# Moving the local branch of an E-Branchformer layer from a phase of its own into the attention loop

## The chip, the cores and the metric

The kernel runs on one core of one Trainium2 chip. The metric is device time in microseconds of one execution. TensorE's clock is not constant: the records show it either granted in full (1.0) or at half (0.5).

## The reference, cut to what matters

The reference is one E-Branchformer layer, forward and all gradients, for 2 batches of 4000 tokens of width 144 in bf16.

```python
xa = _layernorm(x)
q, k, v = split(xa @ w_qkv)
glob = softmax(q @ k.T * D**-0.5) @ v @ w_att_out        # attention branch, 4000 x 4000 scores
h = _gelu(xa @ w_mlp_in)                                 # local branch
u, g = h[..., :D], h[..., D:]
g = _layernorm(g)
gc = sum(pad(g)[:, i:i+T] * dw_csgu[i] for i in range(5)) # depthwise convolution over tokens
loc = (u * gc) @ w_mlp_out
# ... the branches are merged, a second depthwise convolution, a residual;
# jax.vjp of all this, with grad_out, gives the gradients of x and of seven weights
```

## The kernel before

The two batches run one after the other, each in four phases: `phase_in` (norm of x, transposes, Q, B, which carries the gradient into the scores, and the whole local branch, forward and backward), `phase_attn` (scores, exp, and everything that needs the 4000 x 4000 matrices), `phase_merge_out` and `phase_dx`. `finish_weights` closes the kernel. Tokens are in 32 row blocks of 128.

In `phase_in` the local branch runs in groups of four row blocks, pipelined over groups:

```python
def norm4(dst, src, rs, tag):
    ... bn_stats, bn_aggr (VectorE); rs = pow(var + eps, -0.5) (POOL); nm = -mean * rs (VectorE)
    for j in range(4):
        nc.scalar.activation(dst[:, j, :], src[:, j, :], ACT.Identity, bias=nm[:, j:j + 1], scale=rs[:, j:j + 1])
def stB(g):
    ... # products for hs, sq = hs**2; Q; B; dug
    nc.gpsimd.tensor_scalar(a_[:], sq[:], K0 * K1, K0, op0=ALU.mult, op1=ALU.add)
    nc.vector.tensor_tensor(a_[:], a_[:], hs[:], op=ALU.mult)
    nc.scalar.activation(a_[:], a_[:], ACT.Tanh)
    ... # h, norm4(gn_t), and the gelu gradient gp_t on VectorE and POOL
def stC(g): ...  # forward convolution pc (TensorE), gc, dgc, ug; tap gradients into their own PSUM bank dW
def stD(g): ...  # backward convolution, norm gradient, dh
for s in range(NGR + 5):
    stA(s); stB(s - 1); stC(s - 3); stD(s - 5)      # bounds checks cut
```

In `phase_attn` a *unit* is a row block's quarter: 1000 keys. TensorE runs in program order; the other engines' orders are chosen by a scheduler.

```python
NP, NT = 4, 2                                        # P and Sm kept for four rows; transposes PT, ST for two
ps_s: 1 x [128, 2, 512]; ps_d: 3 banks; ps_x: 2; ps_y: 1      # all eight PSUM banks
def unit(i, c2):
    pS, pD = ...                                      # eight products of 500 columns
    nc.scalar.activation(pd, pS[:, :, 0:SC], ACT.Exp, accum_out=...)          # one exp of 1000 columns
    for h in range(2):
        nc.vector.scalar_tensor_tensor(Sm[...], pD[h][:, 0:SC], 1.0, P[...], op0=ALU.mult, op1=ALU.mult, accum_out=...)
# between units, on TensorE: y and z of row i-2 (from PT, ST) and the column sums X of a finished pair of rows
```

Of the kernel before, what the change touches and what calls it, by code (L numbers as in the profile page):

```python
# [14 lines left out]
D = 144  # L15
DR = 16
# [1104 lines left out]
def weights(k):  # L1121
# [7 lines left out]
    with tc.tile_pool(name="w_tmp", bufs=1) as tp_, tc.tile_pool(name="w_ps", bufs=2, space=PSUM) as ps:  # L1129
# [9 lines left out]
        W.Wqkv = load_k(k.w_qkv, D, 3 * D, "w_qkv_s", nc.sync)  # L1139
        W.Wo = load_k(k.w_att_out, D, D, "w_o_s", nc.scalar)  # L1140
# [3 lines left out]
        Wmh = wp.tile([128, 2, 2, D], BF, name="w_mh")  # L1144
# [4 lines left out]
        W.Wmh = Wmh  # L1149
# [40 lines left out]
        W.WoT = transpose_k(W.Wo, D, 0, D, "w_oT")  # L1190
        WlT = transpose_k(Wl, D, 0, D, "w_lT")
        WiT = transpose_k(Wi, D, 0, 2 * D, "w_iT", tp_)
        W.WmT = wp.tile([128, 2, 2, D], BF, name="w_mT")
        nc.vector.memset(W.WmT[:, :, 1, :], 0.0)
        for h in range(2):
            for cc in range(2):
                w = 128 if cc == 0 else DR
                for kt in range(2):
                    rk = 128 if kt == 0 else DR
                    pt = ps.tile([128, 128], BF, tag="tp")  # L1200
                    nc.tensor.transpose(pt[0:w, 0:rk], Wmh[0:rk, h, kt, cc * 128:cc * 128 + w], ident[0:rk, 0:rk])
                    nc.vector.tensor_copy(W.WmT[0:w, h, cc, kt * 128:kt * 128 + rk], pt[0:w, 0:rk])
# [64 lines left out]
        W.WvoT = wp.tile([128, 2, D], BF, name="w_voT")  # L1267
        W.Wvo = wp.tile([128, 2, D], BF, name="w_vo")
        for t, l, r in ((W.WvoT, W.Wo, WvT), (W.Wvo, WvT, W.Wo)):
            nc.vector.memset(t[:, 1, :], 0.0)  # L1270
            for mt in range(2):
                mw = 128 if mt == 0 else DR
                fused(lambda kt: l[:, kt, :], two(r), 1.0, mt * 128, mw, t[0:mw, mt, :])
        W.Wl = wp.tile([128, 2, D], BF, name="w_l")
        nc.vector.tensor_copy(W.Wl[:], Wl[:])

        W.UT = [W.WvoT, WlT]
        W.U = [W.Wvo, W.Wl]
# [5 lines left out]
        for h in range(2):  # L1284
            A = tp_.tile([128, 2, 5, D], BF, name="w_A%d" % h)
            Bz = tp_.tile([128, 2, 5, DR], BF, name="w_Bz%d" % h)
            for kt in range(2):
                for kk in range(5):
                    nc.vector.tensor_scalar(A[:, kt, kk, :], W.UT[h][:, kt, :], W.wm[:, h, kt, kk:kk + 1], None, op0=ALU.mult)
                    nc.vector.tensor_scalar(Bz[:, kt, 4 - kk, :], Wmh[:, h, kt, 128:D], W.wm[:, h, kt, kk:kk + 1], None, op0=ALU.mult)  # L1290
# [16 lines left out]
            for kt in range(2):  # L1307
                nc.tensor.matmul(pt[0:80, 0:D], Bz[:, kt, :, :].rearrange("p a b -> p (a b)"), W.UT[h][:, kt, :], start=(kt == 0), stop=(kt == 1))
# [81 lines left out]
def phase_in(k, W, b, S):  # L1390

    nc, tc = k.nc, k.tc
    with ExitStack() as es:
        pp = es.enter_context(tc.tile_pool(name="in_big", bufs=1))
        ld = es.enter_context(tc.tile_pool(name="in_ld", bufs=2))
        wk = es.enter_context(tc.tile_pool(name="in_wk", bufs=2))
        sm = es.enter_context(tc.tile_pool(name="in_sm", bufs=4))
        ps_t = es.enter_context(tc.tile_pool(name="in_pst", bufs=2, space=PSUM))
        ps_2 = es.enter_context(tc.tile_pool(name="in_ps2", bufs=1, space=PSUM))
        ps_1 = es.enter_context(tc.tile_pool(name="in_ps1", bufs=2, space=PSUM))  # L1400
        ps_w = es.enter_context(tc.tile_pool(name="in_psw", bufs=1, space=PSUM))
        R = pp.tile([128, NBK * 128], BF, name="xaR")
        goT = main_arr(k, pp, "goT")
        gnT = main_arr(k, pp, "gnT")
        st80 = pp.tile([128, 2 + NBK * 128 + 2], BF, name="st80")
        gn80 = Rows80(k, pp, st80, 64, "gn80", 4)
        dgcT = main_arr(k, pp, "dgcT")
        dgc80 = Rows80(k, pp, st80, 96, "dgc80", 4)
        dW = ps_w.tile([128, 2, 512], F32, name="dW")
        go80, dug, h_t, gn_t, gp_t, dh_t, dgc_t = {}, {}, {}, {}, {}, {}, {}  # L1410
        rstd = {}
        nc.gpsimd.memset(S.B_t[:, 31, :], 0.0)
        id_ = W.ident

        def norm4(dst, src, rs, tag):

            mv = sm.tile([128, 4, 2], F32, tag="mv" + tag, name="mv")
            for j in range(4):
                st = sm.tile([128, 6], F32, tag="st", name="st")
                nc.vector.bn_stats(st[:], src[:, j, :])  # L1420
                nc.vector.bn_aggr(mv[:, j, :], st[:])
            ve = sm.tile([128, 4], F32, tag="ve" + tag, name="ve")
            nc.gpsimd.tensor_scalar(ve[:], mv[:, :, 1], EPS, 1.0, op0=ALU.add, op1=ALU.mult)
            nc.gpsimd.tensor_tensor(rs, ve[:], W.mhalf[:], op=ALU.pow)
            nm = sm.tile([128, 4], F32, tag="nm" + tag, name="nm")
            nc.vector.scalar_tensor_tensor(nm[:], mv[:, :, 0], -1.0, rs, op0=ALU.mult, op1=ALU.mult)
            for j in range(4):
                nc.scalar.activation(dst[:, j, :], src[:, j, :], ACT.Identity, bias=nm[:, j:j + 1], scale=rs[:, j:j + 1])

        def stA(g):  # L1430
# [4 lines left out]
            norm4(S.xaa[:, g * 4:g * 4 + 4, :], xg, S.rstd_x[:, g * 4:g * 4 + 4], "x")  # L1435
            pm = ps_t.tile([128, 4, 128], BF, tag="tp")
            for j in range(4):
                nc.tensor.transpose(pm[:, j, :], S.xaa[:, g * 4 + j, 0:128], id_[:])
            nc.scalar.copy(S.xaT[:, g * 512:(g + 1) * 512], pm[:].rearrange("p a b -> p (a b)"))
            pr = ps_t.tile([128, 4, 128], BF, tag="tp")  # L1440
            for j in range(4):
                nc.tensor.transpose(pr[:, j, :], S.xaa[:, g * 4 + j, 16:D], id_[:])
            nc.vector.tensor_copy(R[:, g * 512:(g + 1) * 512], pr[:].rearrange("p a b -> p (a b)"))
# [9 lines left out]
            go80[g] = wk.tile([128, 512], BF, tag="go80", bufs=3, name="go80")  # L1453
            nc.vector.tensor_copy(go80[g][0:80, :], pr[0:80].rearrange("p a b -> p (a b)"))

        def stB(g):
            dug[g] = wk.tile([128, 4, D], BF, tag="dug", bufs=4, name="dug")
            h_t[g] = wk.tile([128, 4, 2 * D], BF, tag="h_t", bufs=4, name="h_t")
            gn_t[g] = wk.tile([128, 4, D], BF, tag="gn_t", bufs=6, name="gn_t")
            gp_t[g] = wk.tile([128, 4, 2 * D], BF, tag="gp_t", bufs=5, name="gp_t")  # L1460
            rstd[g] = sm.tile([128, 4], F32, tag="rstd", bufs=6, name="rstd")
            hs = wk.tile([128, 4, 2 * D], BF, tag="hs")
            sq = wk.tile([128, 4, 2 * D], BF, tag="sq")
            o8 = go80.pop(g)
            for hf in range(2):
                i0 = g * 4 + hf * 2
                js = slice(hf * 2, hf * 2 + 2)
                ph = ps_2.tile([128, 2, 512], F32, tag="w", name="ph")
                for q in range(2):
                    i = i0 + q  # L1470
                    ti = slice(i * 128, (i + 1) * 128)
                    nc.tensor.matmul(ph[:, q, 0:2 * D], S.xaT[:, ti], W.Wi2[:, 0, :], start=True, stop=False)
                    nc.tensor.matmul(ph[:, q, 0:2 * D], R[:, ti], W.Wi2[:, 1, :], start=False, stop=True)
                nc.scalar.copy(hs[:, js, :], ph[:, :, 0:2 * D])
                nc.scalar.activation(sq[:, js, :], ph[:, :, 0:2 * D], ACT.Square)  # L1475
# [7 lines left out]

                pb = ps_2.tile([128, 2, 512], F32, tag="w", name="pb")
                for q in range(2):
                    i = i0 + q
                    for m in range(5):
                        nc.tensor.matmul(pb[:, q, 0:2 * D], goT[:, i * 128 + m:i * 128 + m + 128], W.GL[:, m, :, :].rearrange("p a b -> p (a b)"), start=(m == 0), stop=False)  # L1488
                    nc.tensor.matmul(pb[:, q, 0:2 * D], o8[0:80, (hf * 2 + q) * 128:(hf * 2 + q + 1) * 128], W.GL80[0:80, :, :].rearrange("p a b -> p (a b)"), start=False, stop=True)
                nc.vector.tensor_copy(dug[g][:, js, :], pb[:, :, D:2 * D])  # L1490
                if i0 + 1 < 31:
                    nc.scalar.copy(S.B_t[:, i0:i0 + 2, :], pb[:, :, 0:D])
                else:
                    nc.scalar.copy(S.B_t[:, i0, :], pb[:, 0, 0:D])
                    nc.scalar.copy(S.B_t[0:LASTR, i0 + 1, :], pb[0:LASTR, 1, 0:D])

            h_ = h_t[g]
            a_ = wk.tile([128, 4, 2 * D], BF, tag="a_")
            nc.gpsimd.tensor_scalar(a_[:], sq[:], K0 * K1, K0, op0=ALU.mult, op1=ALU.add)
            nc.vector.tensor_tensor(a_[:], a_[:], hs[:], op=ALU.mult)  # L1500
            nc.scalar.activation(a_[:], a_[:], ACT.Tanh)
            q_ = a_
            nc.vector.tensor_scalar(q_[:], q_[:], 0.5, 0.5, op0=ALU.mult, op1=ALU.add)
            nc.vector.tensor_tensor(h_[:], q_[:], hs[:], op=ALU.mult)
            norm4(gn_t[g], h_[:, :, D:2 * D], rstd[g], "g")
            t3 = wk.tile([128, 4, 2 * D], BF, tag="t3", bufs=1)
            nc.gpsimd.tensor_scalar(t3[:], sq[:], 6 * K0 * K1, 2 * K0, op0=ALU.mult, op1=ALU.add)
# [581 lines left out]
```

## Time and profile before

| | before |
|---|---|
| time, median of 4 runs | 1727.53 us (1727.04 to 1728.07) |
| `phase_in`, batch 0 / batch 1 | 207 / 215 us |
| `phase_attn`, batch 0 / batch 1 | 463 / 464 us |
| merge, dx (batch 0) | 96, 50 us |
| `finish_weights` | 56 us |
| one row block in the attention's steady part | 13.84 us |

The first view gives busy time by stretch of the run, before. The columns are the stretch and its length in us, then busy time and instruction count of TensorE, its weight loads, VectorE, ScalarE and POOL, the mean granted TensorE clock, the share of the DMA engines and GB/s.

```profile
core 0: us, PE busy (x) PEld busy (x) DVE busy (x) ACT busy (x) POOL busy (x), PEclk, DMA share, GB/s
40.00:247.00 207.00, 124.10 (x1037) 91.46 (x1036) 111.29 (x345) 96.35 (x240) 110.85 (x120) 0.73 0.26 80
247.00:710.00 463.00, 445.73 (x5189) 325.82 (x5188) 255.27 (x798) 205.11 (x419) 85.48 (x168) 0.96 0.84 147
306.00:666.00 360.00, 350.19 (x4238) 263.15 (x4235) 208.17 (x654) 167.52 (x343) 69.56 (x137) 1.00 0.89 153
```

In 40 to 247 us (`phase_in`) no engine is busy over 60% of the time and the clock is 0.73: the phase waits on its own chains. In 306 to 666 us (steady attention) TensorE is busy 350.19 of 360 us at clock 1.00: it is the bound.

The next view lists what TensorE waited for, before, over the whole run (us in total, times, longest):

```profile
PE pm L1364 <- ACT gn_t L1428: 61.7, 16, 4.8
...
PE X L1706 <- POOL Qs L1673: 16.2, 30, 0.9
...
PE X L1707 <- DVE Bt L1676: 8.8, 32, 1.6
...
PE pS L1645 <- ACT Pm L1653: 5.0, 14, 0.4
PE pt L1921 <- DVE f_ET L1890: 4.8, 1, 4.8
```

The first line lies in `phase_in` and the last in `finish_weights`; the three between lie in the attention, 30 us in two batches. (Among the lines left out, one of 23.0 us for `QB` lies before the first exp of the two batches.) From the page, the busy tenths of TensorE and its granted clock in 40 slices, before:

```profile
PE   6666649999999999876556665999999999987653
PEclk9777757999999999987776776799999999998775
```

The two stretches of 5 to 7 are the two `phase_in`, and the clock is down there too.

### The profile page before, as it was taken

The page shows a single profiled execution, that of the slowest core. Times are in us where ns is not written, and L with a number is a line of the kernel's source. Part 1 is how long each engine was busy: PE and PEld are TensorE (multiplying, and loading weights), DVE is VectorE, ACT ScalarE, POOL GpSimd, SP SyncE. Part 2 cuts the span into 40 slices and gives each one's busy share as a digit, 9 for nine tenths or more (in the row PEclk, how much of TensorE's full clock was granted, in tenths as well). Part 3 has the DMA queues.
Part 4 walks back from the last instruction along what each step waited for, and adds up shares of the span by engine and source line. Part 5 has one row for each costly group of instructions (what it writes and reads, how often), then busy time and mean ns, then how long its engine had stood idle before and what let it go on. Part 6 is the DMA issues. An engine that isn't in the chain of part 4 may idle for free. (4 is left out here: it accounts for less than half of the span.)

```text
span 1734.3 us, 38321 instructions
## 1 busy us (share of the span) xinstructions
PE 1385.7 (80%) x15302; PEld 1041.7 (60%) x15302; DVE 897.0 (52%) x3070; ACT 674.1 (39%) x1499; POOL 490.1 (28%) x799
## 2 busy tenths in 40 slices
PE   6666649999999999876556665999999999987653
PEld 3345425777777777776435452577777777776631
DVE  4466634555555556213736563456555555621393
ACT  4555423444444444101245542344444444410120
POOL 1556431121221211102755553112122121110260
PEclk9777757999999999987776776799999999998775
DMA  3222218898988889534423221888889988854320
GB/s 91 70 83 85 75 52 146 147 156 145 163 149 164 151 147 154 135 108 110 110 68 94 83 76 58 146 147 156 152 158 149 160 153 149 154 132 118 97 52 11
DMA packets 631408, 206.32 MB, mean 119 GB/s; under 512 B 592628, under 2 KB 627124, under 8 KB 631220
## 3 DMA queue, kind: packets, MB, share of 16 engines
q1 hardware_dynamic: 630356, 203.69, 58.4%
q8 instruction: 122, 2.00, 0.5%
q14 instruction: 66, 0.54, 0.1%
q10 hardware_dynamic: 864, 0.09, 0.0%
HBM read 49.28 MB, written 14.43 MB: 37 GB/s over the span
## 5 line engine op out<-in xcount | busy, mean ns | idle before, releaser
L1656 DVE SCALAR_TENSOR_TENSOR Sm<-pD,Pm 128x500 bf16<-128x500 f32 x512 | 327.1, 677 | 357.6 <-ACT Pm L1653 357.6
L1653 ACT ACTIVATE Pm<-pS 128x1000 bf16<-128x1000 f32 x256 | 255.9, 1000 | 286.9 <-PE pS L1648 282.1
L1706 PE MATMUL X<-Qs,Sm 128*128 128x144 bf16 x2048 | 298.2, 226 | 16.7 <-POOL Qs L1673 16.2
L1707 PE MATMUL X<-Bt,Pm 128*128 128x144 bf16 x2048 | 295.2, 226 | 8.8 <-DVE Bt L1676 8.8
L1707 PEld LDWEIGHTS <-Pm 128*128 128x128 bf16 x2048 | 200.2, 98 | 48.3 <-issue 20.8
L1706 PEld LDWEIGHTS <-Sm 128*128 128x128 bf16 x2048 | 200.5, 98 | 41.6 <-issue 13.8
L1648 PE MATMUL pS<-xaT,QTm 128*128 128x500 bf16 x512 | 160.8, 397 | 0.0
L1650 PE MATMUL pD<-xaT,BTm 128*128 128x500 bf16 x512 | 158.3, 392 | 0.0
L1688 PE MATMUL y<-xaa,PT 128*128 128x144 bf16 x2048 | 150.9, 228 | 0.8 <-DVE B_t L1696 0.8
L1688 PE MATMUL y<-xaa,ST 128*128 128x144 bf16 x2048 | 148.9, 226 | 0.0
L1688 PEld LDWEIGHTS <-PT 128*128 128x128 bf16 x2048 | 134.4, 99 | 1.0 <-issue 1.0
L1688 PEld LDWEIGHTS <-ST 128*128 128x128 bf16 x2048 | 132.5, 98 | 0.0
L1669 POOL TENSOR_SCALAR nd<-dd,rl 128x1 f32<-128x1 f32 x64 | 17.1, 267 | 348.9 <-DVE rl L1665 348.9
L1645 PE MATMUL pD<-XR,QBr 16*128 16x500 bf16 x512 | 112.1, 395 | 1.9
L1712 POOL TENSOR_TENSOR acc_2860<-xs,acc_2860 128x432 f32<-128x432 f32 x48 | 52.9, 1102 | 203.7 <-ACT xs L1711 203.7
L1712 POOL TENSOR_TENSOR acc_14637<-xs,acc_14637 128x432 f32<-128x432 f32 x48 | 52.9, 1102 | 202.5 <-ACT xs L1711 202.5
L1645 PE MATMUL pS<-XR,QBr 16*128 16x500 bf16 x512 | 103.2, 396 | 6.4 <-ACT Pm L1653 5.0
L1650 PEld LDWEIGHTS <-BTm 128*128 128x128 bf16 x512 | 52.0, 102 | 64.4 <-issue 10.1
L1488 PE MATMUL pb<-w_GL,goT 128*128 128x288 bf16 x320 | 69.4, 355 | 16.4 <-ACT sq L1475 16.4
L1714 DVE TENSOR_TENSOR acc_2860<-X,acc_2860 128x432 f32<-128x432 f32 (+1 forms) x128 | 74.8, 584 | 12.2 <-PE X L1707 12.1
L1714 DVE TENSOR_TENSOR acc_14637<-X,acc_14637 128x432 f32<-128x432 f32 (+1 forms) x128 | 74.8, 584 | 12.2 <-PE X L1707 12.1
L1711 ACT COPY xs<-X 128x432 f32<-128x432 f32 x96 | 49.5, 516 | 79.9 <-PE X L1707 75.9
(963 smaller groups left out, 2719.4 us busy)
## 6 DMA issues: line engine op xcount, KB each, us to landing
gs<-in_grad_out_dram SPq DMA_DIRECT2D x24, 720.0 KB
gtap<-gn_d_493 SPq DMA_DIRECT2D x8, 720.0 KB
gtap<-gn_d_12270 SPq DMA_DIRECT2D x8, 720.0 KB
gs<-in_grad_out_dram SPq DMA_DIRECT2D x8, 540.0 KB
xg<-in_x_dram SPq DMA_DIRECT2D x28, 144.0 KB
dh_d_496<-dh SPq DMA_DIRECT2D x8, 288.0 KB
dh<-dh_d_496 SPq DMA_DIRECT2D x8, 288.0 KB
dh_d_12273<-dh SPq DMA_DIRECT2D x8, 288.0 KB
```

Of the source, the lines that this page charges most:

```text
L1488: nc.tensor.matmul(pb[:, q, 0:2 * D], goT[:, i * 128 + m:i * 128 + m + 128], W.GL[:, m, :, :].rearrange("p a b -> p (a b)"), start=(m == 0 ...
L1645: nc.tensor.matmul(o_, QBr[rr, bi, :], S.XR[rr, c2, 0:SC], start=True, stop=False)
L1648: nc.tensor.matmul(pS[:, h, 0:SC], QTm[:, bi, :], S.xaT[:, c0 + h * SC:c0 + (h + 1) * SC], start=False, stop=True)
L1650: nc.tensor.matmul(pD[h][:, 0:SC], BTm[:, bi, :], S.xaT[:, c0 + h * SC:c0 + (h + 1) * SC], start=False, stop=True)
L1653: nc.scalar.activation(pd, pS[:, :, 0:SC], ACT.Exp, accum_out=st["l", i][:, c2:c2 + 1])
L1656: nc.vector.scalar_tensor_tensor(Sm[:, pb, c1:c1 + SC], pD[h][:, 0:SC], 1.0, P[:, pb, c1:c1 + SC], op0=ALU.mult, op1=ALU.mult, accum_out=s ...
L1688: nc.tensor.matmul(y[:, w, :], src[:, tb, j, :], S.xaa[:, j, :], start=(j == 0), stop=(j == NBK - 1))
L1706: nc.tensor.matmul(X[:, jj, :], Sm[:, pb, j * 128:(j + 1) * 128], Qs[:, pb, :], start=(kk == 0), stop=False)
L1707: nc.tensor.matmul(X[:, jj, :], P[:, pb, j * 128:(j + 1) * 128], Bt[:, pb, :], start=False, stop=(kk == 1))
L1711: nc.scalar.copy(xs[:, 0:nj, :], X[:, 0:nj, :])
L1712: nc.gpsimd.tensor_tensor(a_, xs[:, 0:nj, :], a_, op=ALU.add)
L1714: nc.vector.tensor_tensor(a_, X[:, 0:nj, :], a_, op=ALU.add)
```

## The change

The intent is to hide the local branch. `phase_in` shrinks to `phase_head` (norm, transposes, Q, B), and the local branch becomes a list of small steps, each for a pair of row blocks, run between the units of the attention, where VectorE and ScalarE have time to spare. To make room, P and Sm are kept for three rows, the transposes and the exps are made by halves, and the PSUM of the scores is cut to single banks so that one bank, `f`, is left for all local steps and for the just-in-time transposes (`jit`) of Q and B. Also to make room, weights and sums that only `finish_weights` needs go to DRAM and are read back there.

```diff
-def phase_in(k, W, b, S):      # stA, stB, stC, stD over groups of four row blocks
+def phase_head(k, W, b, S):    # only stA, stT, stB: x and grad_out transposes, Q, B; dug goes to DRAM
...
+def local_steps(k, W, b, S, es, ps):          # ps: the one-bank pool "f"
+    def pR(p): ...   # TensorE transposes into f, ScalarE copies R
+    def pH(p, j): ...  # products into f, ScalarE copies hs and squares sq
+    def pG(p): ...   # POOL, VectorE, tanh, norm, pow, gn scaling, gelu gradient: one uncut chain
+    def pC(p): ...   # forward convolution into f, ScalarE gc, VectorE dgc, du, ug, dh
+    def pW(q, half): ... # tap gradients into f, VectorE adds them to SBUF
+    def pD(p): ...   # backward convolution into f, ScalarE dgf, VectorE and POOL: norm gradient
+    R7 = 7
+    for p in range(NBK // 2):
+        t = R7 * p
+        ev += [(t, pR, (p,)), (t + 1, pH, (p, 0)), (t + 2, pH, (p, 1)), (t + 2.5, pG, (p,)),
+               (t + 9, lambda p: gnC.put(p, gn_t[p]), (p,)), (t + 14, ld_dug, (p,)), (t + 18, pC, (p,)),
+               (t + 21, lambda p: dgC.put(p, dgc_t[p]), (p,)), (t + 31, pD, (p,))]
+    for q in range(NGR):
+        ev += [(2 * R7 * q + 24, ld_tap, (q,)), (2 * R7 * q + 31.4, pW, (q, 0)), (2 * R7 * q + 32.4, pW, (q, 1))]
...
 def phase_attn(k, W, b, S):
-    NP, NT = 4, 2
+    NP = 3
-        ps_s = ...(name="at_pss", bufs=1)     # [128, 2, 512]
-        ps_d = ...(name="at_psd", bufs=3)
+        ps_s = ...(name="at_pss", bufs=2)     # single banks
+        ps_d = ...(name="at_psd", bufs=2)
+        ps_f = ...(name="at_psf", bufs=1)
...
-                nc.scalar.activation(pd, pS[:, :, 0:SC], ACT.Exp, ...)          # 1000 columns
+                for h in range(2):
+                    nc.scalar.activation(P[:, pb, c1:c1 + SC], pS[h][:, 0:SC], ACT.Exp, ...)   # 500 columns
...
+                    while ev and ev[0][0] < 4 * i + c2 + 1:      # after each unit: the local steps that are due
+                        _, fn, a = ev.pop(0)
+                        fn(*a)
```

The times of the steps are in units, seven per pair. Taken modulo seven, `gnC.put` (9) falls into the unit of the second `pH` (2), `dgC.put` (21) into that of `pR` (0), and `pW` (31.4, 32.4) into those of `pD` (3) and `pC` (4): two users of the one bank in one unit.

## The prediction

> **What bounds the kernel now.** Busy time by stretch gives the stages, once per batch: phase_in 40–247 us and 856–1071, attention 247–710 and 1071–1535, then merge and dx. In attention's steady part (306–666 us) TensorE is busy 350 of 360 us at clock 1.00; one row block takes 13.84 us (starts of the QTm matmuls). VectorE is 58% busy, ScalarE 47%, DMA engines 89%; SyncE spends 4.9 us issuing each of two transposes per row. Attention is bound by TensorE. phase_in is bound by latency: no engine above 61%, clock 0.73.
>
> **What moves.** phase_in keeps the x and grad_out transposes, Q and B: per group of four blocks an estimated 5 us of ScalarE (from 496, 580, 410 ns and smaller copies), 4 of VectorE, 4–8 of TensorE by its clock. I expect 80 us in place of 207 and 215: about -260 us.
>
> The local branch moves into attention. TensorE, at the trace's 62 ns for 144 columns and an estimated 0.12 us for 288: about +51 us per batch, fully on the path: +102 us. Floor per row 15.4 us. Finish re-reads weights and sums from DRAM: +5.
>
> ScalarE and VectorE rise to an estimated 78% and 83% of that floor (exp by halves adds a start and a 0.2 us accumulator read, four times per row). No table switches: exp and tanh share a set (the Trainium skill, "ScalarE: Activation LUTs", Table sets); the trace agrees, one table load in all.
>
> **The catch.** Both pS and both pD buffers serve one unit, so the next unit waits for exp and the Sm products: chain about 2.6 us against about 3 us of other TensorE work. ScalarE and VectorE are strict FIFO (the Trainium skill, "TensorE: Matmul & The Clock Gate", Architectural detail); no record in this trace contradicts it. In the changed order tanh, the GELU chain on VectorE and POOL, the norm's pow (1.0 us) and the gn scaling on ScalarE all stand between two consecutive units' exps, in 12 of 16 pairs per batch. Before, tanh to last gn took 9.9–11.7 us for four blocks; for two I estimate 6. The next exp is ready after about 2, so TensorE loses about 4 us per pair. The local PSUM tile has one buffer, and two local steps share some units (put then H; put then R; conv then tap gradient): the second waits for evacuation, 2–3 us per pair. The gradient chain through POOL: about 1. Together about 6 us × 32 pairs: about +180 us, and TensorE may fall to half clock after the longest gaps.
>
> **Sum.** 1727 - 260 + 102 + 5 = 1574 without stalls; with them about 1755 us. 80% range 1655–1865. Faster by over 2%: 0.25; within 2%: 0.23; slower: 0.52.
>
> **What would show each step.** phase_in replaced by about 80 us of head. Steady attention: 18–19.5 us per row instead of 15.4, TensorE about 80% busy. Its waits: exp and Sm of the unit before, evacuation of the local PSUM tile. ScalarE idle before gn_t, waiting for VectorE's nm, some 4 us per pair, with exps directly behind. If the row takes 15.4–16 us and these waits are small, the catch is wrong. Merge, dx unchanged.
>
> **What would make it wrong.** POOL's chain may be shorter at half size, or stalls of one cause may hide another's: then about 1620–1660. SyncE (9.8 us of transposes plus about 3.9 of local DMAs per row) could bind, delaying the neighbour rows that the convolutions read: slower still. The head may take 70 or 100 us.

## The result, and the profile after

The changed kernel took 1808.93 us (median of 4 runs, 1800.61 to 1812.99), the kernel before 1727.53 us. The ratio is 1.0465, 95% interval 1.0427 to 1.0503: slower.

| stage, us in the profiled runs | before | after |
|---|---|---|
| `phase_in` / `phase_head`, batch 0 | 207 | 45 |
| attention, batch 0 | 463 | 657 |
| merge, dx, batch 0 | 96, 50 | 88, 48 |
| `phase_in` / `phase_head`, batch 1 | 215 | 62 |
| attention, batch 1 | 464 | 657 |
| merge, dx, batch 1 | 94, 49 | 90, 48 |
| `finish_weights` | 56 | 76 |

The heads gave 315 us, 55 more than forecast; attention took 387 us more, where the forecast had 282; `finish_weights` took 20 more. The same view of busy time by stretch, after:

```profile
40.00:85.00 45.00, 35.58 (x363) 28.73 (x361) 20.23 (x89) 28.19 (x83) 15.22 (x28) 0.96 0.31 92
85.00:742.00 657.00, 544.48 (x5960) 394.31 (x5957) 358.40 (x1144) 321.73 (x952) 237.65 (x463) 0.91 0.68 125
200.00:660.00 460.00, 368.02 (x4128) 272.89 (x4127) 254.10 (x806) 229.50 (x678) 172.51 (x340) 0.93 0.67 124
1735.00:1811.00 76.00, 24.47 (x106) 9.05 (x106) 26.38 (x124) 8.57 (x36) 2.81 (x4) 0.50 0.17 50
```

In the steady part (200 to 660 us) TensorE is busy 368 of 460 us, 80%, and the clock is 0.93, no longer 1.00. One row block takes about 21 us. VectorE is busy 55% of the time, the DMA engines 67%. So nothing is saturated: TensorE waits, and runs slowly after waiting. What it waited for, after:

```profile
PE pw L1622 <- ACT dgf L1641: 42.2, 16, 5.0
PE ph L1562 <- DVE gnC L1506: 33.2, 30, 2.2
PE pc L1532 <- ACT dgf L1641: 31.8, 8, 4.5
PE pr L1554 <- DVE dgC L1506: 28.8, 26, 2.2
PE pt L2022 <- DVE f_ET L1991: 20.9, 1, 20.9
...
PE pj L1708 <- ACT dgf L1641: 11.7, 4, 3.6
PE X L1784 <- POOL Qs L1754: 9.8, 8, 1.5
...
PE pD L1722 <- DVE Sm L1732: 8.1, 17, 2.8
PE pt L2023 <- DMA f_ETr<-f_E_26716: 7.4, 1, 7.4
```

`pw`, `ph`, `pc`, `pr`, `pj` are all users of the bank `f`; each waits until the one before has been copied out (`dgf`, `gnC`, `dgC` are those copies). The two lines of `pt` lie in `finish_weights`. The page's rows that answer to those shown of before:

```profile
PE   6798877887888789767588877888787878976723
PEclk9969998999898999998786998899899989998855
```

How a copy comes to be late is seen in one pair of the first batch. The timeline of ScalarE, after (start, duration, instruction, idle time before it and what ended it):

```profile
267.85 0.38 ACT L1641 ACTIVATE dgf<-pc,rstd 128x144 bf16<-128x144 f32 x1 [0.99 <-PE pc L1533]
...
272.15 0.90 ACT L1405 ACTIVATE gn_t<-h_t,nm,rstd 128x144 bf16<-128x144 bf16 x2 [3.84 <-DVE nm L1403]
272.97 0.56 ACT L1731 ACTIVATE Pm<-pS 128x500 bf16<-128x500 f32 x1
...
273.53 0.57 ACT L1731 ACTIVATE Pm<-pS 128x500 bf16<-128x500 f32 x1
...
274.09 0.37 ACT L1641 ACTIVATE dgf<-pc,rstd 128x144 bf16<-128x144 f32 x1
```

VectorE in the same stretch:

```profile
266.97 1.24 DVE L1580 TENSOR_SCALAR a__3967<-a__3967 128x576 bf16<-128x576 bf16 x1
...
270.62 0.46 DVE L1588 TENSOR_TENSOR oq<-oq,t_3987 128x576 bf16<-128x576 bf16 x1 [0.81 <-POOL oq L1587]
271.96 0.16 DVE L1403 SCALAR_TENSOR_TENSOR nm<-mv,rstd 128x2 f32<-128x2 f32 x1 [0.88 <-POOL rstd L1401]
...
273.65 0.68 DVE L1732 SCALAR_TENSOR_TENSOR Sm<-pD,Pm 128x500 bf16<-128x500 f32 x1 [0.94 <-ACT Pm L1731]
```

And TensorE:

```profile
268.04 0.60 PE L1726 MATMUL pS<-xaT,QTm 128*128 128x500 bf16 x2
...
268.90 1.16 PE L1767 MATMUL y<-xaa,ST 128*128 128x144 bf16 x16
274.60 0.59 PE L1532 MATMUL pc<-w_dg,gnC 128*128 128x128 bf16 x4 [4.54 <-ACT dgf L1641]
```

The first half of `dgf` left ScalarE at 268.2 us; then ScalarE stood 3.84 us before `gn_t`, which waited for VectorE's `nm`, which waited for POOL's `pow` (`rstd`). Two exps, whose scores were ready at 268.6 us, started only behind it, from 272.97 us on, and the second half of `dgf` came behind them. Until that was copied, the bank `f` was full and TensorE did not start the next convolution: 4.54 us. A delay is charged to whatever TensorE needs next, which would explain why the list of waits names `f` more than exp: the five users of `f` shown add up to 148 us, exp to 5.3. In this stretch neither ScalarE nor VectorE passes a waiting instruction, as the Trainium skill, "TensorE: Matmul & The Clock Gate", Architectural detail, has it ("ACT/DVE are strict FIFO"). VectorE's first line is a second lengthening: this operation took 1.24 us beside a POOL addition of 1.10 us, in 10 of 32 pairs, and 0.30 us in the other 22, in which no POOL instruction ran beside it. The Trainium skill, "SBUF — State Buffer", Who interferes with whom, says that VectorE in its two-port modes and POOL share a pair of ports and that the loser fully blocks; the trace agrees with it: in all ten the addition had started 0.03 us earlier, and the operation ended 0.17 us after it. These collisions are 9 us of VectorE time in all, and none is left in e2, e3, e5, e6 or e10; e5, without any, is the slowest of these kernels, so they are not the main cause; what they are worth in a gain as small as that of e6 is not separated.

### The profile page after: what moved, and what is told of

It reads as the page before. It is cut to its first block, busy times and chain, and to the rows that moved or that the text cites. A ratio compares the mean times of both kernels' runs of the same rounds, so it can differ in the third digit from the quotient of the medians.

```text
span 1811.2 us, 41290 instructions
## 1 busy us (share of the span) xinstructions
PE 1401.6 (77%) x15366; PEld 1046.6 (58%) x15366; DVE 917.6 (51%) x3245; ACT 770.1 (43%) x2247; POOL 601.8 (33%) x1179
## 5 line engine op out<-in xcount | busy, mean ns | idle before, releaser
L1731 ACT ACTIVATE Pm<-pS 128x500 bf16<-128x500 f32 x512 | 295.1, 583 | 138.8 <-PE pS L1726 136.7
L1784 PE MATMUL X<-Qs,Sm 128*128 128x144 bf16 x2048 | 316.5, 236 | 9.8 <-POOL Qs L1754 9.8
L1785 PE MATMUL X<-Bt,Pm 128*128 128x144 bf16 x2048 | 315.4, 236 | 6.0 <-DVE Bt L1757 5.4
L1790 POOL TENSOR_TENSOR acc_14480<-xs,acc_14480 128x432 f32<-128x432 f32 x80 | 88.2, 1102 | 248.2 <-ACT xs L1789 248.0
L1790 POOL TENSOR_TENSOR acc_1386<-xs,acc_1386 128x432 f32<-128x432 f32 x80 | 88.1, 1101 | 246.4 <-ACT xs L1789 246.4
L1789 ACT COPY xs<-X 128x432 f32<-128x432 f32 x160 | 82.7, 517 | 188.3 <-PE X L1785 184.6
L1722 PE MATMUL pD<-XR,QBr 16*128 16x500 bf16 x512 | 124.9, 412 | 9.1 <-DVE Sm L1732 8.1
L1722 PE MATMUL pS<-XR,QBr 16*128 16x500 bf16 x512 | 116.0, 414 | 6.6 <-ACT Pm L1731 5.3
L1731 ACT ACTIVATION_READ_ACCUMULATOR Pm<-pS 128x1 f32 x512 | 102.9, 201 | 0.0
L1726 PEld LDWEIGHTS <-QTm 128*128 128x128 bf16 x512 | 29.7, 99 | 86.1 <-issue 86.1
L1792 DVE TENSOR_TENSOR acc_1386<-X,acc_1386 128x432 f32<-128x432 f32 x96 | 55.5, 578 | 42.1 <-PE X L1785 42.0
L1792 DVE TENSOR_TENSOR acc_14480<-X,acc_14480 128x432 f32<-128x432 f32 x96 | 55.5, 578 | 40.6 <-PE X L1785 40.5
```

What stands on the lines that cost most here:

```text
L1722: nc.tensor.matmul(o_[:, 0:SC], QBr[rr, bi, :], S.XR[rr, c2, 0:SC], start=True, stop=False)
L1726: nc.tensor.matmul(p_[h][:, 0:SC], w_[:, bi, :], S.xaT[:, c0 + h * SC:c0 + (h + 1) * SC], start=False, stop=True)
L1731: nc.scalar.activation(P[:, pb, c1:c1 + SC], pS[h][:, 0:SC], ACT.Exp, accum_out=ld8[:, 0, n:n + 1])
L1784: nc.tensor.matmul(X[:, jj, :], Sm[:, i % NP, j * 128:(j + 1) * 128], Qs[:, i % 4, :], start=(kk == 0), stop=False)
L1785: nc.tensor.matmul(X[:, jj, :], P[:, i % NP, j * 128:(j + 1) * 128], Bt[:, i % 4, :], start=False, stop=(kk == 1))
L1789: nc.scalar.copy(xs[:, 0:nj, :], X[:, 0:nj, :])
```

## The experiments

The theory from the trace was this. (T) Local chains that cross engines stand uncut in front of exps, Sm products and copies out of `f` (the *chains*), and the steps that share a unit wait for each other's copies (the *bank*); TensorE then loses clock after the gaps. The expectations call the chains A1 and the bank B. The rivals: (R1) the restructured attention itself (three rows, halves, single banks) is slower; (R2) the scheduler's order is bad, and the program's order would do (in the expectations of e3 and e4, R2 is another rival, that ScalarE and VectorE are simply too loaded; the gains of e3, e4 and e7 speak against it); (R3) SyncE's DMA queue is late; no TensorE wait of any size names a DMA in the attention after, so it got no run of its own.

All numbers of the "in attention" columns are read from the traces: the time from the first exp to the last of a batch, TensorE's idle time within it, and the time at half clock within it (means of the two batches).

| kernel | median us | ratio | first to last exp | idle | at half clock | us per row |
|---|---|---|---|---|---|---|
| before | 1727.5 | | 442.8 | 15.5 | 34.7 | 13.84 |
| after | 1808.9 | 1.0465 | 627.4 | 104.7 | 117.9 | 21.0 |
| e1 restructured only | 1714.3 | 0.992 | 438.6 | 3.6 | 30.8 | 13.74 |
| e2 steps spread | 1729.5 | 1.0015 | 582.7 | 71.1 | 86.8 | 19.4 |
| e3 chains cut | 1719.9 | 0.9945 | 581.1 | 72.1 | 68.5 | 19.2 |
| e4 both | 1630.3 | 0.9441 | 531.4 | 38.6 | 39.6 | 17.3 |
| e5 kept order, uncut | 1916.9 | 1.1104 | 678.5 | 143.6 | 160.0 | 22.4 |
| e6 gn scaling later | 1799.7 | 1.0428 | 619.6 | 95.6 | 109.9 | 20.6 |
| e10 only gelu chain cut | 1782.2 | 1.0308 | 615.4 | 88.0 | 103.6 | 20.7 |
| e7 both, and X banks for two users | 1594.3 | 0.9233 | 516.8 | 25.7 | 42.1 | 16.3 |
| e8 e1 with idle gaps | 1939.6 | 1.1231 | 551.1 | 74.7 | 143.0 | 17.6 |
| e9 the same gaps, filled | 1865.1 | 1.0802 | 513.7 | 19.2 | 29.3 | 16.3 |
| e11 e1 with shorter idle gaps | 1863.5 | 1.0798 | 509.6 | 53.6 | 75.2 | 16.1 |
| e12 the shorter gaps, filled | 1826.8 | 1.0574 | 492.3 | 16.6 | 29.6 | 15.6 |

Ratios are to the kernel before on the same chip in the same rounds (medians there 1726.4 to 1727.7). All outputs were correct.

### e1: the restructured attention alone

The kernel before, with the changed attention, and no local steps in it (`phase_in` stays).

```diff
-        ev = local_steps(k, W, b, S, es, ps_f)
+        ev = []
```

> The kernel before, with the changed kernel's attention but no local step in it (local branch still in phase_in): P for three row blocks, exp by halves, transposes by halves, one pD buffer less, 5 of 11 X sums on POOL, the row transposes in a PSUM bank of their own. Theory A (the loss of the change is waits that the local steps bring): attention stays at 460 to 470 us per batch, total 1715 to 1745. Rival R1 (the restructured attention is itself slower: more exp starts, fewer pD buffers, transposes that hold SyncE): attention at 510 us or more per batch, total above 1820.

Measured: 1714.31 us, ratio 0.992 (0.9903 to 0.9937), just under the range of theory A. TensorE's idle time in the attention falls to 3.6 us. R1 falls: three rows, halves and single banks are even a little better. All of the loss comes with the local steps.

### e2: the steps spread so that the large users of the bank are in units of their own

```diff
-               (t + 9, gnC.put ...), (t + 14, ld_dug, (p,)), (t + 18, pC, (p,)),
-               (t + 21, dgC.put ...), (t + 31, pD, (p,))]
+               (t + 12, gnC.put ...), (t + 20, ld_dug, (p,)), (t + 25, pC, (p,)),
+               (t + 27, dgC.put ...), (t + 38, pD, (p,))]
-        ... ld_tap 14q + 24, pW 14q + 31.4 and 32.4
+        ... ld_tap 14q + 30, pW 14q + 36 and 37
```

> The changed kernel with the local PSUM steps moved in time, so that of seven units only the tap gradient's share a unit with another local step (every second pair) and put/H and put/R no longer do. Theory B (one PSUM tile, two users in a unit): TensorE's waits of H for the gn copy and of R for the dgc copy (62 us over both batches in the changed kernel) vanish, and part of those of the tap gradient; total 1720 to 1755. Theory A1 alone (ScalarE and VectorE queues blocked by the GELU and norm chain): these waits only move, since ScalarE still holds the next exp behind gn; total 1785 to 1810.

Measured: 1729.48 us, 79 less than after. The waits of `ph` for `gnC` and of `pr` for `dgC` are gone from the list; the wait of `pc` for `dgf` stays, 27.8 us. The bank is one cause, worth 79 us, 2.5 us per pair. (Moving the steps also moves their copies in ScalarE's queue; e7, below, changes the bank alone.)

### e3: the chains cut

`pG` is cut into five parts, a unit apart, so that each part finds its input ready; `pC` and `pD` get their VectorE work 2.5 and 4.5 units after their convolutions. ScalarE and VectorE are kept in program order, so that the scheduler can't undo it.

```diff
-(t + 2.5, pG, (p,)),
+(t + 2.5, g1, (p,)), (t + 3.5, g2, (p,)), (t + 4.5, g3, (p,)), (t + 5.5, g4, (p,)), (t + 6.5, g5, (p,)),
-(t + 18, pC, (p,)),  (t + 31, pD, (p,))
+(t + 18, pC, (p,)), (t + 20.5, pC2, (p,)),  (t + 31, pD, (p,)), (t + 35.5, pD2, (p,)), (t + 36.5, pD3, (p,))
-        with tc.manual_schedule(engines={PE}):
+        with tc.manual_schedule(engines={PE, Activation, DVE}):
```

> The changed kernel with its times of TensorE steps, but the chains of the local branch cut into pieces that are emitted one unit apart, and ScalarE and VectorE kept in that order: no instruction that waits for POOL's or another engine's slow step stands between two units' exps or Sm products. Theory A1 (blocked queues): ScalarE's wait of about 3.8 us before gn_t goes, and the conv's wait for dg (4.5 us, every second pair) goes; two thirds of the TensorE idle time goes with it and the half-clock windows become few; total 1660 to 1710. Theory B alone: 1790 to 1810. If both engines are simply too loaded (rival R2): no gain, 1790 or more.

Measured: 1719.94 us, 89 less than after, but 10 above the range expected. TensorE's idle time fell by a third, from 105 to 72 us, where two thirds were expected, and half clock by 49 us, to 68: the waits that are left, e3, are large:

```profile
PE ph L1562 <- DVE gnC L1506: 40.4, 30, 2.6
PE pr L1554 <- DVE dgC L1506: 34.3, 26, 2.7
...
PE pw L1655 <- ACT dgf L1672: 23.4, 16, 2.0
```

They are those of the shared bank, which this run does not touch; the 31.8 us of `pc` for `dgf` are gone. The chains are the other cause; that it is the cuts and not the kept order which gain is shown by e5.

### e4: both

> Both: chains cut, and the local PSUM steps spread. If A1 and B are the two causes: attention near the TensorE floor of about 515 us plus some 20 us per batch, total 1570 to 1630, faster than both kernels. If the engines' load binds (R2) or SyncE's queue does (R3): above 1700.

Measured: 1630.25 us, ratio 0.9441 (0.9415 to 0.9468), 179 less than after: the sum of 79 and 89, with some 10 us on top. It lies at the upper end of the range expected, and is faster than the kernel before. The list of waits, e4:

```profile
PE pw L1657 <- ACT sq L1565: 18.1, 12, 2.2
...
PE pD L1765 <- DVE Sm L1775: 12.0, 46, 1.0
PE pw L1655 <- ACT sq L1565: 11.0, 12, 1.0
PE pj L1751 <- POOL QB L1747: 9.4, 2, 4.7
```

What is left are again users of `f` in one unit (the two `pw` fall into the units of the two `pH`, and wait for their `sq`).

### e5: the control for e3, the order kept and nothing cut

```diff
-        with tc.manual_schedule(engines={PE}):
+        with tc.manual_schedule(engines={PE, Activation, DVE}):
```

> The changed kernel with nothing moved, only TensorE, ScalarE and VectorE all kept in the order of the program text, so that each local chain stands uncut between two units' exps. It is the control for the run with cut chains, which kept the same three engines in order. If cutting the chains is what gained 89 us there: no gain here, 1790 to 1860 us, steady rows 20.5 to 22 us. If it was only the kept order that helped (the scheduler having put the exps badly): about 1720 us, as with the cut chains.

Measured: 1916.91 us, 108 more than after and 57 above the range expected. The expectation had the right sign only. R2 falls the other way round: the scheduler's order is the better one, it had already moved part of the chains apart (ScalarE stands idle before `gn_t` for 129.8 us here, for 96.8 us in after). In this kernel the chain shows itself openly, as waits of the scores for exp, e5:

```profile
PE pS L1722 <- ACT Pm L1731: 74.3, 20, 5.5
PE pw L1622 <- ACT dgf L1641: 61.6, 16, 8.5
```

### e6: only the gn scaling moved, on ScalarE

```diff
-    for j in range(n):                       # inside norm_rows
-        nc.scalar.activation(dst[:, j, :], ...)
+    return scale                             # called two units later, at t + 4.5
-        with tc.manual_schedule(engines={PE}):
+        with tc.manual_schedule(engines={PE, Activation}):
```

> The changed kernel with one step moved on ScalarE alone: the gn scaling (two instructions per pair) two units later, and ScalarE kept in program order; tanh and all of VectorE's chain stay between two units. If ScalarE's first-in-first-out queue, the exp standing behind a gn scaling that waits for POOL and VectorE, is the larger part of what the cut chains gained (89 us): 1720 to 1760 us. If VectorE's queue in front of the Sm products counts as much, or the wait only moves to another instruction: 1770 to 1810 us. Waits of the third conv step for dgf should stay either way, as the gradient chain is not touched.

Measured: 1799.72 us, 9 less than after. The groups by line, for `gn_t`, after (count, then busy us and mean ns, then idle time of ScalarE before it and what ended it):

```profile
L1405 ACT ACTIVATE gn_t<-h_t,nm,rstd 128x144 bf16<-128x144 bf16 x64 | 29.5, 500 | 96.8 <-DVE nm L1403 96.8
```

and e6:

```profile
L1406 ACT ACTIVATE gn_t<-h_t,nm,rstd 128x144 bf16<-128x144 bf16 x64 | 28.9, 500 | 0.0
```

This is the instructive miss. After, ScalarE stood 96.8 us idle before `gn_t`, 3.0 us per pair; e6 takes all of it away, and gets 9 us. A second miss: the waits of `pc` and `pj` for `dgf`, 43.5 us in after, were expected to stay and are gone from the list, so a wait's length there is not what removing it gains. TensorE's wait for Sm rose from 8.1 to 28.6 us, and VectorE still stands idle for 23.4 us behind the same `pow`: the exps were no longer stuck on ScalarE, but the Sm products still were on VectorE. Two other things are not separated in these 9 us: e6 also keeps ScalarE in program order, which may cost something, and the collisions with POOL are gone. That a chain has to be cut on every engine that it passes is what e6 suggests; e10 cuts the same chain on both.

### e10: only the gelu and norm chain cut, on both engines

As e3, without the cuts of `pC` and `pD`.

> The changed kernel with only the GELU and norm chain cut into five parts, one unit apart; the gradient steps after the convolutions stay in one piece, and TensorE, ScalarE and VectorE keep program order, as in the uncut control (1917 us) and the run with all chains cut (1720 us). If the GELU chain is what stands in the way of the exps: 1720 to 1780 us, and the waits of the score products for exp (74 us in the control) are gone. If the gradient steps behind the convolutions count as much: 1800 to 1860 us, with the waits of the tap gradient for dgf still about 60 us.

Measured: 1782.18 us, between the two ranges expected. The waits of the scores for exp fall from 74.3 to 16.0 us, and those of `pw` for `dgf` from 61.6 to 23.4 us, the figure of e3, though the gradient steps are uncut. Against the uncut control (e5) the gelu chain is worth 135 us, 4.2 per pair; cutting the gradient steps as well (e3) is worth 62 more, 1.9 per pair. Against the scheduler's order (after), e10 gains only 27; that is a net figure, as e10 also gives up the scheduler's order of the gradient steps. So the gelu chain is the larger one, and the scheduler had already hidden part of it; how much is not measured by itself.

### e7: the best version

e4, with the `jit` transposes and the tap gradients using the two banks of X in place of `f`.

```diff
-            pj = ps_f.tile([128, 4, 128], BF, tag="f", name="pj")
+            pj = ps_x.tile([128, 4, 128], BF, tag="x", name="pj")
-        pw = ps.tile([128, 384], F32, tag="f", name="pw")
+        pw = psx.tile([128, 384], F32, tag="x", name="pw")
```

> The version with chains cut and steps spread (1630 us), with the just-in-time transposes and the tap gradient taking their PSUM tile from the two banks of the row sums X in place of the one bank of the local steps. If the single bank shared by neighbours is what is left between its 17.3 us per row and the floor of about 15.4: the waits of tap gradient for the square (29 us in all) and of transposes (9 us) go, 16.0 to 16.5 us per row, 1575 to 1605 us. If the X banks are as busy and the wait only moves to X: 1620 to 1650 us, with new waits of X for ScalarE.

Measured: 1594.34 us (1591.96 to 1597.32), ratio 0.9233 (0.9214 to 0.9252), 16.3 us per row. That is the change's intent, fulfilled: 7.7% below the kernel before. What TensorE still waits for, e7:

```profile
PE pc L1533 <- DMA dgC<-dgC: 19.6, 6, 4.6
...
PE pD L1765 <- DVE Sm L1775: 12.6, 48, 1.0
...
PE X L1827 <- POOL Qs L1797: 7.0, 15, 1.6
```

The first is new: at 16.3 us per row the neighbour rows that the backward convolution reads are late 6 times, up to 4.6 us.

### e8 and e9: what a gap costs beyond its length

After runs 118 us per batch at half clock, before 35. Whether that is a cost beside the gaps, or only their shadow, can't be read from one trace. So e1, whose steady part has clock 1.00, was given 18 gaps per batch: TensorE reads a tile, POOL overwrites it with three multiplications, TensorE reads it again. In e8 it waits; in e9 it runs 15 useless products of 500 columns meanwhile. The instruction orders of the other engines are identical.

```diff
+        def gap(n):
+            nc.tensor.matmul(gf[:, 0:64], zz[:, 0:128], zz[:, 0:64], start=True, stop=True)
+            for _ in range(3):
+                nc.gpsimd.tensor_tensor(zz[:], zc[:], zc[:], op=ALU.mult)
+            for _ in range(n):                       # 0 in e8, 15 in e9
+                nc.tensor.matmul(gf[:, 0:500], W.ident[:], S.xaT[:, 0:500], start=True, stop=True)
+            nc.tensor.matmul(gf[:, 0:64], zz[:, 0:128], zz[:, 0:64], start=True, stop=True)
+        ev = [(7 * p + 3.5, gap, (n,)) for p in range(18)]
```

> The kernel with the attention restructured and no local steps inside (1714 us, TensorE at full clock in the steady part), in which TensorE is made to wait 18 times per batch, once every seven units, for a chain of three POOL multiplications of 128x512 that starts when TensorE reaches that place (estimated 3.4 us and some latency, so about 3.7 us of idle each, 133 us in all). If a gap costs only its length: 1830 to 1860 us, and the same as the run with the gap filled. If each gap is followed by a window of half clock, as the traces of the changed kernel look, some 1.7 us more for each of the 36: about 1890 to 1920 us, and half clock in the attention's records rises from 31 to about 90 us per batch.

> The same kernel with the same waits at the same places, but TensorE runs 15 products of 500 columns (estimated 3.1 us, results unused) while POOL works, so it waits no longer for the chain and is hardly idle. The order on ScalarE, VectorE, POOL and SyncE is the same as in the idle run. If the half clock after gaps is a cost of its own: about 45 to 65 us less than the idle run, with the clock at 1.00 in the steady part. If it is none: the two agree within 10 us.

Measured: 1939.63 and 1865.07 us. The idle run is 75 us above the filled one, 2.1 us for each of 36 gaps of 3.9 us. Busy time by stretch in the steady part, e8:

```profile
300.00:740.00 440.00, 380.79 (x4175) 279.94 (x4173) 195.27 (x585) 193.49 (x566) 138.91 (x204) 0.90 0.71 123
```

and e9:

```profile
300.00:740.00 440.00, 422.70 (x4691) 299.56 (x4688) 208.29 (x626) 207.75 (x607) 149.30 (x218) 1.00 0.77 132
```

The clock is 0.90 against 1.00. In the clock records of e8, all but one of the gaps that did not already lie in half clock are followed by a half-clock window, mostly of 6.8 us. Both runs were slower than expected, their difference is 10 us over the range expected, and half clock rose to 143 us per batch where about 90 was expected, as most windows were twice as long; three POOL multiplications in the loop delay other things too, but equally in both. The half clock costs time of its own: 114 us more of it per batch cost 37 us, 0.33 us per us. (Less than 0.5, because part of a window lies in the gap or in time when TensorE waits anyway; that reason is argued, not measured.)

### e11 and e12: the same with two multiplications

> As the idle-gap run, with two POOL multiplications in place of three, so that TensorE stands idle some 2.5 us at 18 places per batch, a length like most of the changed kernel's longer gaps, in place of 3.9. With the gap filled instead: see the other run. If gaps of this length also bring a window of half clock each: 60 to 80 us above the filled run. If only gaps over about 3 us do: within 20 us of it. If some do, by where they fall: between.

> The same two POOL multiplications and places, with 10 products of 500 columns (an estimated 2.1 us) on TensorE in the wait. From the filled run with three multiplications (1865 us) less 36 times some 1.1 us: 1815 to 1835 us, clock 1.00 in the steady part.

Measured: 1863.45 and 1826.79 us, 37 us apart: 1.0 us for each gap of 2.7 us, less than the 60 to 80 expected if every gap brought a window, more than the 20 if only gaps over 3 us did. Of the gaps of 2.0 to 2.6 us outside half clock, 11 were followed by a window and 11 not; of the eight of 3.2 us, 5 were. From the first-to-last-exp times, the rate is 0.38 us per us of half clock.

### Idle time and half clock together

With 0.33 us for each us of half clock, carried over from e8 and e9, two terms give most of the differences of the first-to-last-exp times from after; they miss by 1 to 9 us, and in the two smallest changes, e6 and e10, the half-clock term does not improve the sum:

| | idle, change | half clock, change x 0.33 | sum | measured |
|---|---|---|---|---|
| e2 | -33.5 | -10.2 | -43.7 | -44.8 |
| e3 | -32.6 | -16.3 | -48.9 | -46.4 |
| e4 | -66.1 | -25.8 | -91.9 | -96.0 |
| e5 | +38.9 | +13.9 | +52.8 | +51.1 |
| e6 | -9.1 | -2.6 | -11.7 | -7.8 |
| e10 | -16.6 | -4.7 | -21.4 | -12.1 |
| e7 | -79.0 | -25.0 | -104.0 | -110.6 |

## Why the prediction was right or wrong

The verdict, slower, and the range held the result; the forecast of the change did not. It said +28 us; +81 was measured. Point by point:

- **"Attention is bound by TensorE ... phase_in is bound by latency."** Right. The heads left behind took 45 and 62 us.
- **"I expect 80 us in place of 207 and 215: about -260 us."** Too pessimistic: -315. This error of 55 us hid part of the larger one, by luck: without it the result would have stood at the upper edge of the range.
- **"About +51 us per batch, fully on the path."** About right. By the table above, after against e1 is 188.8 us, of which 101.1 are idle and 29 half clock; the rest, 59 us, is TensorE's local work and what the sum misses. The same subtraction for e7, where the other two terms are small, leaves 52.
- **"Together about 6 us × 32 pairs: about +180 us."** Right in size for idle time: TensorE's idle time in the attention rose by 89 us per batch, 178 in both. The list of causes was right too, though of the waits that it named those of the bank hold nearly all, and exp and Sm only 5.3 and 8.1 us; spreading the steps gained 2.5 us per pair (forecast 2 to 3). For the chains, e5 shows the forecast of 4 us per pair for a chain that really stands uncut (4.2, and ScalarE idle before `gn_t` 129.8 us in all). But after is not e5: in its order the scheduler had set part of the work apart, and against it e10 gains 27 us. The gradient chain, forecast at 1 us per pair, was worth 1.9 (e10 to e3). That the sum came out right is in part luck: two errors nearly cancel.
- **"TensorE may fall to half clock after the longest gaps."** This is the step that failed: the mechanism stood in the text and was given no term in the sum. Half clock rose by 83 us per batch (after against before); at the 0.33 to 0.38 us per us measured in e8, e9 and e11, e12 that is an estimated 27 to 32 us per batch, some 55 to 63 us in all. The gaps before it were not only the longest: in after's own trace 6 of 10 gaps of 2.0 to 2.6 us were followed by a window, and all 16 of 3.4 us and more.
- **"18–19.5 us per row ... TensorE about 80% busy."** Busy 80%, but 21.0 us per row. The busy share hid the loss: a TensorE at half clock counts as busy. Share and clock have to be read together.
- **Exp and tanh share a table set.** Right: the trace of after, too, has one table load in all (the Trainium skill, "ScalarE: Activation LUTs", Table sets).
- **"SyncE ... could bind."** It did not: no wait of TensorE for a DMA of any size stands in the attention after.
- **"Finish re-reads weights and sums from DRAM: +5."** It took 20 us more, a second term too small. TensorE waited 20.9 us for `f_ET` in place of 4.8: it is made from sums whose load was issued behind the weights' and landed 8.6 us after its own issue, at 1748.3 us, and were then added for 1.97 us. A second wait, for `f_ETr`, took 7.4 us; it is 0.2 us in e1, whose finish is that of before.
- **"Merge, dx unchanged."** They were 15 us shorter in all. But the attention keeps working for 30 us after its last exp in place of 20, to bring the last local steps home.

In stages: the forecast of the profiled change, 25 us without rounding, missed by +105 in attention, -53 in the heads, +15 in finish and -15 in merge and dx; together +52. Of the 105, an estimated 55 to 63 are half clock and about 20 the tail of local steps. Of the 20 to 30 that remain about 15 come with the restructured attention: TensorE is busy 435 us between a batch's first and last exp in e1, 427 us in before. The rest is not taken apart further.

## What to carry to other kernels

Before work is moved into the shadow of a bound engine, ask of every chain that crosses engines where each piece stands in its queue, and cut it on every engine that it passes: moving one piece of the gelu chain on ScalarE alone gained 9 us, cutting that chain on ScalarE and VectorE 27, and cutting the gradient steps too 89. A spare bank shared by steps that fall into one slot is a second queue, and moving the steps to slots of their own gained 79 us; with both, the same change turned from 4.7% slower to 5.6% faster, and with a further bank for two of the steps to 7.7% faster. When a forecast has TensorE idling in gaps of 2 us and more, give the half clock after them a term of its own, here about half of the gap's length for gaps near 4 us (2.1 us for 3.9), and less for shorter ones (1.0 us for 2.7).

## What the Trainium skill lacked or had wrong

- "TensorE: Matmul & The Clock Gate", HAM oscillation, gives the rule "no PE-idle gaps >~3.4µs". Shorter gaps are not safe here: those of 2.0 to 2.6 us were followed by half clock in 11 of 22 cases (e11), and gaps of about 1.7 us in 6 of 8 cases (e9 and e12). Gaps of 3.4 us and more always were, but for one. The lengths of the windows after these gaps, 3.4 us or twice that, agree with the window of 3413 ns that the page gives under "What's actually happening".
- The section on HAM oscillation reckons the cost of half clock as half the throttled time. Filled against idle gaps measured 0.33 (e8, e9) and 0.38 (e11, e12) of it.
- "DMA: Bandwidth & Descriptors", Issuing engines are not separate DMA queues, calls the time to initiate a DMA "usually small relative to the DMA itself". For transposing DMAs from SBUF to SBUF it is not small here: SyncE's records show a median of 4.9 us for issuing one of 128x4096, and 1.9 and 2.4 us (the two tensors) for one of 128x2048. Two per row before are 9.8 us of SyncE in a row of 13.8 us. The landing of a transfer is not in these traces; an estimate is 6.0 us each (in before's steady part SyncE's DMA queue kept the 16 engines busy 88.2% of 360 us, with 53 transposes issued), so that issuing takes about four fifths as long.
- No page gives a time for POOL's `pow`; the traces show 1.01 us for 128x4 elements and 0.71 us for 128x2, so a tiny tensor halved is far from half the time. It is one of the links that make the chain long.
